# One expert's tokens turned by TensorE instead of by DMA, and its weight splits moved back, in a clustered attention with a mixture of experts

## The chip, the cores and the metric

The kernel runs on one core of a Trainium2 chip, as one launch. The metric is the device time of an execution in microseconds. A core has TensorE (products of matrices, results in PSUM), VectorE, ScalarE and GpSimd (in the profile DVE, ACT and POOL), SyncE (SP), which issues most DMAs here, and 16 DMA engines. Each engine works through its own instructions in order; they meet by semaphores.

## The reference

Two parts in a row. First attention for 2 batches, 8 heads, 768 positions and 64 columns. Each query and key is given to the nearest of 16 centroids, and a query sees only keys of its own cluster:

```python
mask = q_assign[:, :, :, None] == k_assign[:, :, None, :]
scores = np.where(mask, scale * np.matmul(q, k.transpose(0, 1, 3, 2)), -1e9)
attn = softmax(scores)                 # along the keys
x = (attn @ v) as (2, 768, 512)        # the heads side by side
```

Then a mixture of 8 experts, one for each token, chosen by a gate that can also hand on the choice of the token before:

```python
logits = x @ w_gate                    # 512 -> 8
e = argmax(logits[s]) if s == 0 or local_gate[s] < 0.5 else e of token s-1
h = relu(x[s] @ w1[e])                 # 512 -> 1024
out[s] = softmax(logits[s])[e] * (h @ w2[e])   # 1024 -> 512
```

## The kernel before

**Number format.** Every f32 factor of the second part is split into a high and a low f16 half, and a product is three f16 products (high by high, high by low, low by high) summed in PSUM. So a chunk of weights that a DMA has loaded (`wst`, 128 x 1024 f32, 512 KB) needs a *split*: ScalarE writes the high half (L858), then VectorE the low half (L860, `W<-wst,W`). W1 and W2 of an expert are four chunks each.

**Stages.** Attention fills the first 255 us or so. Its tokens are written to DRAM (`xd`) as pairs of f16 halves, and are routed. Tokens are then sorted by expert: the *lead* is the expert with most tokens in the first batch and is done in two parts (200 and 144 slots), the others follow by rank, in the order 1, 7, 2, 6, 3, 5, 4 (`ORD`), with 296, 144, 272, 168, 224, 184 and 200 slots. For each, `expert` (from L882) gives four kinds of work:

- `gather`: GpSimd fetches the rows of the tokens by indirect DMAs of up to 128 rows (L901, `xg`). They must be turned, columns to partitions (`XT`). For the ranks SyncE does this by a DMA transpose for each block (L906). For the lead's second part TensorE does it, by eight transposes for a block (L914, into `xgt` in PSUM), and ScalarE copies the result (L916): that is `turn`.
- `g1(m)`, eight *hidden blocks*: 12 products each (four rows of weights by three, L927 to L929), then ScalarE writes the high half of the hidden values (`H`, L930) and VectorE the low half (L931). Three PSUM buffers hold them.
- `g2`, the *second products*: for a remainder of tokens in two halves of 48 products (L967 to L969, `g2m` and `g2o`), copied by VectorE (`yt`, L970) and turned back by TensorE (L979); for a full 128 tokens in one unit (L948 to L950).
- `put`: ScalarE scales the result (`ob`, L936) and GpSimd scatters it to the output (L938).

**Order.** The program is written in one order, and a scheduler that plans with times of its own sets the order of each engine from it. Behind the lead's first part the loop over `p` does it: at `p` = 0 the hidden blocks and second products of the lead's second part, and spread among them as `tasks` the four splits of rank 1's W1; each split's `two` also issues the next load (`dma_next`). `POST` = 1 says behind how many units the tasks begin. Five loads are issued ahead of the loop (`NST` = 5, the number of `wst` buffers); the later ones wait until a split has freed a buffer. `issue_after` holds an instruction behind a named one.

In the same stretch VectorE and TensorE also do routing work for tokens that overflow their expert's slots: `hbo`, `rbo` (L782 to L788), the slot masks `loj` (L792) and the small products `po` (L793).

Of the kernel before, what the change touches and what calls it, by code (L numbers as in the profile page):

```python
# [43 lines left out]
NST = 5  # L44
ORD = [1, 7, 2, 6, 3, 5, 4]
# [4 lines left out]
POST = 1  # L50
# [9 lines left out]
CAPS = [296, 272, 224, 200, 184, 168, 144]  # L60
# [3 lines left out]
def tile_kernel(ctx, tc, q, k, v, centroids, w_gate, w_local, w1, w2, out):  # L64
    nc = tc.nc
    V, A, G, PE, SP = nc.vector, nc.scalar, nc.gpsimd, nc.tensor, nc.sync
# [10 lines left out]
    E, DM = w1.shape[0], w1.shape[1]  # L77
    DF = w1.shape[2]
    KD, KF = DM // 128, DF // 128
# [9 lines left out]
    xd = dram.tile([B * S, KD, 2, 128], F16, name="xd")  # L89
# [4 lines left out]
    TM, TX = ("pst" if UNI else "pm"), ("pst" if UNI > 1 else "x")  # L94
# [417 lines left out]
    cmark = {}  # L512
# [366 lines left out]
    def expert(r, cap, src, gi, sci, pr, mp, nbuf, g1pool=None, last=False, gates=None, putm=None, tpe=None):  # L879
# [11 lines left out]
        nb = (cap + 127) // 128  # L891
# [13 lines left out]
                else:  # L905
                    cmark["XT"] = SP.dma_start_transpose(out=st["XT"][:, :, i * 128:i * 128 + n], in_=xg[0:n]).ins  # L906

        def turn():
            for i in range(nb):
                n = min(128, pad - i * 128)  # L910
                pool, tag = tpe[i % 2]
                pt = pool.tile([128, 2 * KD, 128], F16, name="xgt", tag=tag)
                for c in range(2 * KD):
                    PE.transpose(pt[:, c, 0:n], st["xg", i][0:n, c * 128:(c + 1) * 128], rc["ident16"][0:n, 0:n])  # L914
                XT = st["XT"][:, :, i * 128:i * 128 + n]
                A.activation(out=XT, in_=pt[:, :, 0:n], func=AF.Copy)  # L916

        def g1(m):
            def f():
# [34 lines left out]
        def g2_rest(h):  # L954
            def f():
                Hh, W2 = st["H"], W[r, 1]
                sl = slice(nf * 128, cap)
                if h == 0:
                    st["yt"] = mp.tile([128, KD, 192], F32, name="yt", tag="yt", bufs=1)
                y = g2_ps()  # L960
                yv = y.rearrange("p (k c) -> p k c", k=2)
                for k2 in range(2):
                    kk = 2 * h + k2
                    for m in range(KF):
                        lh, ll = (W2[:, x, m, kk * 128:(kk + 1) * 128] for x in range(2))
                        with gate(3 * rest / 2400):
                            PE.matmul(out=yv[:, k2, 0:rest], lhsT=lh, rhs=Hh[:, 0, m, sl], start=(m == 0), stop=False)  # L967
                            PE.matmul(out=yv[:, k2, 0:rest], lhsT=lh, rhs=Hh[:, 1, m, sl], start=False, stop=False)
                            PE.matmul(out=yv[:, k2, 0:rest], lhsT=ll, rhs=Hh[:, 0, m, sl], start=False, stop=(m == KF - 1))  # L969
                mark["V"] = V.tensor_copy(st["yt"][:, 2 * h:2 * h + 2, 0:rest], yv[:, :, 0:rest]).ins  # L970
            return f

# [9 lines left out]
        second = []  # L982
# [4 lines left out]
            fl = [flip(i) for i in range(nf, nb)]  # L987
            second = second[:2] + fl + second[2:] if last else second[:3] + fl + second[3:]
        if tpe:
            return gather, [g1(m) for m in range(KF)], second, turn  # L990
        return gather, [g1(m) for m in range(KF)], second

    if True:
# [182 lines left out]
        for f in ea[2]:  # L1176
            f()
        with tc.issue_after(cmark["flip"]):
            eb[3]()
        att.close()  # L1180
        mp = ctx.enter_context(tc.tile_pool(name="mp", bufs=1, side="right"))
        mpool["b"] = mp
# [5 lines left out]
        def dma_next():  # L1188
            if queue:
                r, kd, i = queue.pop(0)  # L1190
                if (r, 0) not in ws:
                    regs[r] = SP.value_load(rc["eid_i"][0:1, r:r + 1], min_val=0, max_val=E - 1)
                if i == 0:
                    ws[r, kd] = wload(r, kd, lambda: regs[r])
                ws[r, kd][i][0]()
        for i in range(NST):
            dma_next()
        col2 = lambda nm, r: (lambda i: rc[nm][:, BASE[r - 1] + i:BASE[r - 1] + i + 1])

        def two(r, kd, i, gather=None):  # L1200
            ws[r, kd][i][1]()
            with tc.issue_after(gather) if gather else nullcontext():
                dma_next()
        ex = [eb]
        mark["on"] = True
        for p in range(E + 1):
            tasks = []
            if p + 1 < E:
                r = ORD[p]
                ex.append(expert(r, CAPS[r - 1], xd, col2("gi", r), col2("sci", r), col2("pr", r), mp, 2, last=p + 1 == E - 1))  # L1210
                ex[-1][0]()
                first.setdefault("XT", cmark["XT"])
            if 0 < p < E:
                tasks += [lambda i=i, r=ORD[p - 1]: two(r, 1, i, first["XT"]) for i in range(4)]
            if p + 1 < E:
                tasks += [lambda i=i, r=ORD[p]: two(r, 0, i, first["XT"]) for i in range(4)]
            units = []
            if p < E:
                units += ex[p][1]

            if p != 1:
                units += ex[max(p - 1, 0)][2]
            nt = 0
            for i, un in enumerate(units):
                un()
                while nt < len(tasks) and nt < (i + 1 - POST) * len(tasks) / (len(units) - POST):
                    tasks[nt]()
                    nt += 1
                if p == E - 1 and i == 0:
                    last_put = mark["G"]  # L1230
                if p == 0 and i == 1:
                    probs()
                if p == 1 and i == 1:
                    late["pool"] = mp
                    over()
# [45 lines left out]
```

## Time and profile before

| | us |
|---|---|
| three executions | 440.75, 443.43, 553.84 (median 443.43) |
| profiled execution | 440.79 |
| its span, first to last instruction | 439.0 |
| TensorE busy | 383.5 (87%) |
| VectorE, ScalarE, GpSimd busy | 300.6, 249.2, 191.3 |

The span is what the trace covers; about 1.8 us of the execution lie around it. Starts in the rows are in us from the start of the span. In a row of instructions the bracket at its end gives how long the engine was idle before it, and what ended that. "Issue" is a wait for nothing that the profile shows, "remote" one that nothing on the core is seen to end. The attention ends near 256 us, the lead's first part near 276, its second part near 299, and rank 1's products begin at 292.

### The profile page before, as it was taken

The numbers are of one execution on the slowest core, as the hardware profiler recorded it, in microseconds if no ns is written. First come the engines' busy times: TensorE is split into PE (matmuls) and PEld (weight loads), VectorE is DVE, ScalarE is ACT, GpSimd is POOL, SyncE is SP. The second block draws the span as 40 slices with busy tenths as digits, with TensorE's granted clock in tenths as the row PEclk, the third lists the DMA queues.
The fourth block names the chain that finished last, engine by engine and source line by source line (L and its number), as shares of the span: only waits on it lengthen the run. The fifth ranks groups of instructions, "written<-read, shape, count | busy, mean of one in ns | idle before, by whom it ended". The sixth has DMA issues, their size and how long they took to land. (4 is left out here: it accounts for less than half of the span.)

```text
span 439.0 us, 12733 instructions
## 1 busy us (share of the span) xinstructions
PE 383.5 (87%) x5095; PEld 336.9 (77%) x5095; DVE 300.6 (68%) x738; ACT 249.2 (57%) x472; POOL 191.3 (44%) x209
## 2 busy tenths in 40 slices
PE   0288698998979999899989999789999999999980
PEld 0246588887979899798879997576799998988950
DVE  7786667765837769879889258848677875876620
ACT  6257867875756667545765520435457756756520
POOL 3005776967739685455667401432133231202120
PEclk9999889999989999799999999999999999999996
DMA  8899879996598949237691710989799999798210
GB/s 195 148 200 266 208 130 194 192 209 149 124 202 160 192 92 197 49 75 172 180 232 21 152 37 20 331 203 227 259 268 327 296 378 305 244 325 250 88 36 32
DMA packets 123166, 80.84 MB, mean 184 GB/s; under 512 B 92503, under 2 KB 108119, under 8 KB 123104
## 3 DMA queue, kind: packets, MB, share of 16 engines
q1 hardware_dynamic: 120480, 73.01, 69.6%
q0 software_dynamic: 2624, 6.98, 4.8%
q8 instruction: 41, 0.67, 0.6%
q14 instruction: 21, 0.17, 0.1%
HBM read 46.88 MB, written 8.47 MB: 126 GB/s over the span
## 5 line engine op out<-in xcount | busy, mean ns | idle before, releaser
L366 POOL TENSOR_TENSOR lo<-e 128x512 f16<-128x512 f32 x90 | 97.1, 1094 | 76.6 <-ACT e L360 76.4
L328 DVE TENSOR_REDUCE mx<-pm 128x2 f32<-128x512 f32 x144 | 96.0, 685 | 33.4 <-PE pm L326 33.0
L360 ACT ACTIVATE e<-pst 128x512 f32<-128x512 f32 x144 | 81.7, 592 | 32.9 <-PE pst L358 27.9
L860 DVE SCALAR_TENSOR_TENSOR W<-wst,W 128x1024 f16<-128x1024 f32 x64 | 78.1, 1230 | 16.7 <-ACT W L858 14.8
L357 PE MATMUL pst<-Q1T,K1T 128*128 128x256 f16 x288 | 73.6, 279 | 4.6 <-ACT e L360 4.2
L358 PE MATMUL pst<-Q2T,K2T 128*128 128x256 f16 x288 | 72.9, 279 | 0.0
L858 ACT ACTIVATE W<-wst 128x1024 f16<-128x1024 f32 x64 | 66.9, 1055 | 7.3 <-DMA wst<-in_moe_w_dram 7.3
L927 PE MATMUL g<-XT,W 128*128 128x200 f16 (+6 forms) x288 | 67.9, 251 | 2.9 <-DMA XT<-xg 1.8
L928 PE MATMUL g<-XT,W 128*128 128x200 f16 (+6 forms) x288 | 67.9, 251 | 0.0
L326 PE MATMUL pm<-K2T,QMT 128*128 128x256 f16 x288 | 58.0, 294 | 10.8 <-DMA QMT<-QM 7.1
L929 PE MATMUL g<-XT,W 128*128 128x200 f16 (+6 forms) x288 | 65.7, 251 | 0.5 <-DVE W L860 0.5
L385 PE MATMUL o<-VF,e 128*128 128x65 f32 x432 | 58.7, 276 | 0.0
L385 PEld LDWEIGHTS o<-VF,e 128*128 128x128 f32 x432 | 55.5, 198 | 0.8
L930 ACT ACTIVATE H<-g 128x200 f16<-128x200 f32 (+6 forms) x72 | 23.6, 339 | 56.7 <-PE g L929 48.2
L938 POOL DMA_INDIRECT out_dram<-ob,scim x16 | 19.0, 1190 | 72.1 <-ACT W L858 19.2
L388 PE MATMUL o<-VL,e 128*128 128x64 f16 x360 | 47.9, 194 | 0.0
L387 PE MATMUL o<-VH,e 128*128 128x65 f16 x360 | 47.9, 196 | 0.0
L389 PE MATMUL o<-VH,lo 128*128 128x65 f16 x360 | 44.9, 195 | 0.4 <-POOL lo L366 0.4
L326 PEld LDWEIGHTS <-QMT 128*128 128x128 f16 x288 | 24.4, 106 | 18.8 <-issue 8.0
L389 PEld LDWEIGHTS <-lo 128*128 128x128 f16 x360 | 34.2, 99 | 2.6 <-issue 1.5
L387 PEld LDWEIGHTS <-e 128*128 128x128 bf16 x360 | 34.7, 99 | 1.8
L388 PEld LDWEIGHTS <-e 128*128 128x128 bf16 x360 | 34.3, 100 | 1.4
(306 smaller groups left out, 882.8 us busy)
## 6 DMA issues: line engine op xcount, KB each, us to landing
wst<-in_moe_w_dram SPq DMA_DIRECT2D x64, 512.0 KB
xd<-xt SPq DMA_DIRECT2D x12, 384.0 KB
ld_k<-in_k_dram SPq DMA_DIRECT2D x7, 384.0 KB
ld_q<-in_q_dram SPq DMA_DIRECT2D x7, 384.0 KB
ld_v<-in_v_dram SPq DMA_DIRECT2D x7, 384.0 KB
Q1T<-QXT SPq DMA_DIRECT2D x14, 192.0 KB
ld_k<-in_k_dram SPq DMA_DIRECT2D x2, 192.0 KB
ld_q<-in_q_dram SPq DMA_DIRECT2D x2, 192.0 KB
```

What stands on the lines that cost most here:

```text
L326: PE.matmul(out=ps[:, i], lhsT=rg(QMT, u)[:, hh * T + 2 * qp + i, :], rhs=rg(K2T, u)[:, hh * T + 2 * kc:hh * T + 2 * kc + 2, :], start=Tru ...
L328: mark["V"] = V.tensor_reduce(out=st["mx"][:, 2 * qp:2 * qp + 2, kc], in_=ps, axis=AX.X, op=ALU.max).ins
L357: PE.matmul(out=ps[:, i], lhsT=rg(K1T, u)[:, j, :], rhs=rg(Q1T, u)[:, hh * T + 2 * qc:hh * T + 2 * qc + 2, :], start=True, stop=False)
L358: PE.matmul(out=ps[:, i], lhsT=rg(K2T, u)[:, j, :], rhs=rg(Q2T, g)[:, 2 * qc:2 * qc + 2, :], start=False, stop=True)
L360: mark["A"] = A.activation(out=e, in_=ps.rearrange("p a b -> p (a b)"), func=AF.Exp, scale=SCL).ins
L366: G.tensor_tensor(out=lo, in0=e, in1=eh, op=ALU.subtract)
L385: PE.matmul(out=o[:, t, 0:65], lhsT=e[:, sl], rhs=vf[:, hh, j, 0:65], start=first, stop=False, skip_group_check=True)
L387: PE.matmul(out=o[:, t, 0:65], lhsT=eh[:, sl], rhs=vh[:, hh, j, 0:65], start=first, stop=False, skip_group_check=True)
L388: PE.matmul(out=o[:, t, 0:64], lhsT=eh[:, sl], rhs=vl[:, hh, j, :], start=False, stop=False, skip_group_check=True)
L389: PE.matmul(out=o[:, t, 0:65], lhsT=lo[:, sl], rhs=vh[:, hh, j, 0:65], start=False, stop=False, skip_group_check=True)
L860: V.scalar_tensor_tensor(out=l[:, cs], in0=s[:, cs], scalar=WS, in1=h[:, cs], op0=ALU.mult, op1=ALU.subtract)
L927: PE.matmul(out=ps, lhsT=lh, rhs=XT[:, 2 * kk, 0:cap], start=(kk == 0), stop=False)
```

## The change

Rank 1's tokens are turned by TensorE and ScalarE, as the lead's second part's are. Its three blocks (128, 128 and 48 rows) give 24 transposes and three copies. The first block's transposes are placed behind the first half of the second products of the lead's second part, the others behind the second half and its turning back, each held behind the last of the second products issued so far. At `p` = 0 the tasks begin behind six units instead of one. Four loads are issued ahead of the loop, and the first task issues two more; the loads at `p` = 0 are no longer held behind a DMA transpose.

```diff
-        def turn():
-            for i in range(nb):
+        def turn(i):
+            def f():
                 n = min(128, pad - i * 128)
-                pool, tag = tpe[i % 2]
+                pool, tag = tpe[i % len(tpe)]
                 pt = pool.tile([128, 2 * KD, 128], F16, name="xgt", tag=tag)
                 for c in range(2 * KD):
                     PE.transpose(pt[:, c, 0:n], st["xg", i][0:n, c * 128:(c + 1) * 128], rc["ident16"][0:n, 0:n])
                 XT = st["XT"][:, :, i * 128:i * 128 + n]
                 A.activation(out=XT, in_=pt[:, :, 0:n], func=AF.Copy)
+            return f
...
-        for i in range(NST):
+        for i in range(NST - 1):
             dma_next()
...
             ws[r, kd][i][1]()
+            if (r, kd, i) == (ORD[0], 0, 0):
+                dma_next()
...
-                ex.append(expert(r, CAPS[r - 1], xd, col2("gi", r), col2("sci", r), col2("pr", r), mp, 2, last=p + 1 == E - 1))
+                ex.append(expert(r, CAPS[r - 1], xd, col2("gi", r), col2("sci", r), col2("pr", r), mp, 2, last=p + 1 == E - 1, tpe=((ps_x, TX), (ps_m, TM)) if p == 0 else None))
...
-                tasks += [lambda i=i, r=ORD[p]: two(r, 0, i, first["XT"]) for i in range(4)]
+                tasks += [lambda i=i, r=ORD[p]: two(r, 0, i, first.get("XT")) for i in range(4)]
...
+            if p == 0:
+                def held(f):
+                    def h():
+                        with tc.issue_after(cmark["g2"]):
+                            f()
+                    return h
+                tu = [held(f) for f in ex[1][3]]
+                units = units[:9] + tu[:1] + units[9:] + tu[1:]
+            post = POST if p else 6
             nt = 0
             for i, un in enumerate(units):
                 un()
-                while nt < len(tasks) and nt < (i + 1 - POST) * len(tasks) / (len(units) - POST):
+                while nt < len(tasks) and nt < (i + 1 - post) * len(tasks) / (len(units) - post):
```

What the scheduler made of it, at three places. The first is ScalarE at the lead's second part and the start of rank 1; `H<-` with 144 columns is a hidden block of the lead's second part, with 296 one of rank 1, `W_5397<-wst` a split of rank 1's W1. Before:

```order
L930 ACTIVATE H<-g_5435 128x144
L858 ACTIVATE W_5397<-wst 128x1024
L930 ACTIVATE H<-g_5475 128x144
L930 ACTIVATE H<-g_5490 128x144
L858 ACTIVATE W_5397<-wst 128x1024
L930 ACTIVATE H<-g_5509 128x144
L930 ACTIVATE H<-g_5524 128x144
L930 ACTIVATE H<-g_5539 128x144
L858 ACTIVATE W_5397<-wst 128x1024
L930 ACTIVATE H<-g_5558 128x144
L858 ACTIVATE W_5397<-wst 128x1024
L936 ACTIVATE ob<-g2m,prlb_4993 128x512
```

And in the changed kernel, from its seventh hidden block on:

```order
L931 ACTIVATE H<-g_5525 128x144
L858 ACTIVATE W_5397<-wst 128x1024
L931 ACTIVATE H<-g_5547 128x144
L858 ACTIVATE W_5397<-wst 128x1024 x2
L916 ACTIVATE XT<-xgt 128x8x128 x2
L916 ACTIVATE XT<-xgt 128x8x48
L937 ACTIVATE ob<-g2m,prlb_4993 128x512
L937 ACTIVATE ob<-g2o,prlb_5003 16x512
L858 ACTIVATE W_5397<-wst 128x1024
L931 ACTIVATE H<-g_5743 128x296
```

The splits stood behind the second, the fourth, the seventh and the eighth hidden block. Now the first stands behind the seventh, two behind the eighth, and the fourth behind the three new copies and two output copies.

The second is VectorE in the same stretch. Before:

```order
L784 TENSOR_TENSOR rbo<-hbo,tok_489 128x12x19
L788 TENSOR_TENSOR rbo<-hbo,vals_525 128x6x19
L931 SCALAR_TENSOR_TENSOR H<-g_5509,H 128x144
L788 TENSOR_TENSOR rbo<-hbo,vals_525 128x6x19
L788 TENSOR_TENSOR rbo<-hbo,vals_526 128x6x19 x2
L931 SCALAR_TENSOR_TENSOR H<-g_5524,H 128x144
L931 SCALAR_TENSOR_TENSOR H<-g_5539,H 128x144
L860 SCALAR_TENSOR_TENSOR W_5397<-wst,W_5397 128x1024
L931 SCALAR_TENSOR_TENSOR H<-g_5558,H 128x144
L970 COPY yt<-g2m 128x2x144
L970 COPY yt<-g2o 128x2x144
L860 SCALAR_TENSOR_TENSOR W_5397<-wst,W_5397 128x1024
```

In the changed kernel:

```order
L788 TENSOR_TENSOR rbo<-hbo,vals_525 128x6x19 x2
L788 TENSOR_TENSOR rbo<-hbo,vals_526 128x6x19 x2
L932 SCALAR_TENSOR_TENSOR H<-g_5480,H 128x144
L932 SCALAR_TENSOR_TENSOR H<-g_5495,H 128x144
L932 SCALAR_TENSOR_TENSOR H<-g_5510,H 128x144
L932 SCALAR_TENSOR_TENSOR H<-g_5525,H 128x144
L860 SCALAR_TENSOR_TENSOR W_5397<-wst,W_5397 128x1024
L932 SCALAR_TENSOR_TENSOR H<-g_5547,H 128x144
L971 COPY yt<-g2m 128x2x144
L860 SCALAR_TENSOR_TENSOR W_5397<-wst,W_5397 128x1024
L971 COPY yt<-g2o 128x2x144
L860 SCALAR_TENSOR_TENSOR W_5397<-wst,W_5397 128x1024 x2
```

The low half of the fourth hidden block (`g_5490` before, `g_5480` now) has moved behind all `rbo`, and that of the eighth (`g_5558`, `g_5547`) stands behind the first split.

The third is SyncE behind the first loads (`eidi` is the list of experts, read into a register). Before:

```order
L844 DMA wst<-in_moe_w_dram 128x2x512
L906 DMA_TRANSPOSE XT<-xg 128x8x128 x2
L906 DMA_TRANSPOSE XT<-xg 128x8x48
L844 ISA
L844 DMA wst<-in_moe_w_dram 128x2x512
L844 ISA
L844 DMA wst<-in_moe_w_dram 128x2x512
```

In the changed kernel:

```order
L844 DMA wst<-in_moe_w_dram 128x2x512
L1194 TENSOR_LOAD eidi
L1194 ISA x2
L844 ISA
L844 DMA wst<-in_moe_w_dram 128x2x512
L906 DMA_TRANSPOSE XT<-xg 128x8x128
L844 ISA
L844 DMA wst<-in_moe_w_dram 128x2x512
L906 DMA_TRANSPOSE XT<-xg 128x8x16
L844 ISA
L844 DMA wst<-in_moe_w_dram 128x2x512
```

The first row is the fifth load in both. Rank 1's three transposes are gone, and the two of rank 7 (128 and 16 rows) stand between the next loads.

## Rows read from the trace of the kernel before

**Rows 1.** The page: the span, and each engine's busy time, share and instructions.

```profile
span 439.0 us, 12733 instructions
PE 383.5 (87%) x5095; PEld 336.9 (77%) x5095; DVE 300.6 (68%) x738; ACT 249.2 (57%) x472; POOL 191.3 (44%) x209
```

**Rows 2.** By stretch: its length, busy PE, PEld, DVE, ACT, POOL; clock, DMA, GB/s.

```profile
302.00:426.00 124.00, 124.00 (x1466) 109.15 (x1464) 85.18 (x130) 74.41 (x121) 29.59 (x25) 1.00 0.83 257
```

**Rows 3.** The same view, the stretch that the change rewrites.

```profile
280.00:302.00 22.00, 16.83 (x214) 14.31 (x211) 12.23 (x40) 8.06 (x16) 6.88 (x8) 1.00 0.95 237
```

**Rows 4.** TensorE in order of time, 276 to 302: start, duration, line, operation, [idle before].

```profile
276.00 0.90 PE L914 MATMUL xgt<-ident,xg 128*128 128x128 f16 x16
...
279.64 0.46 PE L729 MATMUL pp<-rb,ohlo 128*128 128x32 f16 x12
...
281.01 0.23 PE L929 MATMUL g<-XT,W 128*128 128x144 f16 x1
...
285.17 0.22 PE L967 MATMUL g2m<-H,W 128*128 128x144 f16 x1 [1.58 <-ACT H L930]
...
288.30 0.23 PE L927 MATMUL g<-XT,W 128*128 128x144 f16 x1
...
288.98 0.23 PE L929 MATMUL g<-XT,W 128*128 128x144 f16 x1
...
292.15 0.30 PE L927 MATMUL g<-XT,W 128*128 128x296 f16 x1 [1.82 <-DMA XT<-xg]
...
294.81 0.29 PE L928 MATMUL g<-XT,W 128*128 128x296 f16 x1
...
300.03 0.43 PE L929 MATMUL g<-XT,W 128*128 128x296 f16 x2 [0.48 <-DVE W L860]
...
301.52 0.29 PE L927 MATMUL g<-XT,W 128*128 128x296 f16 x1 [0.31 <-DVE H L931]
```

**Rows 5.** ScalarE in order of time, the same stretch.

```profile
280.06 1.06 ACT L858 ACTIVATE W<-wst 128x1024 f16<-128x1024 f32 x1
284.83 0.47 ACT L930 ACTIVATE H<-g 128x144 f16<-128x144 f32 x2 [3.71 <-remote]
...
299.42 0.69 ACT L936 ACTIVATE ob<-g2m,prlb 128x512 f32<-128x512 f32 x1 [8.93 <-issue]
```

**Rows 6.** VectorE in order of time, 282 to 291.

```profile
282.61 0.17 DVE L609 TENSOR_SCALAR p0m<-pp 128x16 f32<-128x16 f32 x1 [1.65 <-PE g L929]
...
285.16 0.31 DVE L931 SCALAR_TENSOR_TENSOR H<-g,H 128x144 f16<-128x144 f32 x1 [0.47 <-ACT H L930]
...
285.67 0.17 DVE L806 CAST oei<-oe 128x19 int32<-128x19 f32 x1
...
286.28 1.23 DVE L860 SCALAR_TENSOR_TENSOR W<-wst,W 128x1024 f16<-128x1024 f32 x1
...
288.13 0.64 DVE L788 TENSOR_TENSOR rbo<-hbo,vals 128x114 f16<-128x114 f16 x3
...
289.39 1.23 DVE L860 SCALAR_TENSOR_TENSOR W<-wst,W 128x1024 f16<-128x1024 f32 x1 [0.18 <-ACT W L858]
```

**Rows 7.** By stretch again, one us inside the burst of loads and gathers.

```profile
282.00:283.00 1.00, 0.67 (x9) 0.46 (x7) 0.39 (x3) 0.00 (x0) 0.74 (x1) 1.00 1.08 422
```

**Rows 8.** SyncE's DMA issues in order of time: start, time in its queue, count.

```profile
276.09 0.53 SPq L844 DMA_DIRECT2D wst<-in_moe_w_dram  x1
285.97 4.61 SPq L906 DMA_TRANSPOSE XT<-xg  x3
290.84 1.63 SPq L844 DMA_DIRECT2D wst<-in_moe_w_dram  x3
```

**Rows 9.** The tile `xgt`, 260 to 312: durations in ns, shortest/median/longest, and forms.

```profile
L914 PE MATMUL xgt<-ident,xg x16: 164/198/219, 276.0 to 276.7; 128*128 128x128 f16 x8, 16*128 16x16 f16 x8
L916 ACT ACTIVATE XT<-xgt x2: 276/646/1015, 276.9 to 277.8; 128x1024 f16<-128x1024 f16 x1, 128x128 f16<-128x128 f16 x1
```

**Rows 10.** GpSimd in order of time: the next gather that needs a free buffer.

```profile
291.02 0.88 POOL L901 DMA_INDIRECT xg<-xd,gim  x1 [4.29 <-DMA XT<-xg]
```

More of the change, by code (lines that the diff above doesn't have):

```diff
@@ L968, in f @@
                             PE.matmul(out=yv[:, k2, 0:rest], lhsT=lh, rhs=Hh[:, 1, m, sl], start=False, stop=False)
-                            PE.matmul(out=yv[:, k2, 0:rest], lhsT=ll, rhs=Hh[:, 0, m, sl], start=False, stop=(m == KF - 1))
+                            cmark["g2"] = PE.matmul(out=yv[:, k2, 0:rest], lhsT=ll, rhs=Hh[:, 0, m, sl], start=False, stop=(m == KF - 1)).ins
                 mark["V"] = V.tensor_copy(st["yt"][:, 2 * h:2 * h + 2, 0:rest], yv[:, :, 0:rest]).ins
@@ L989, in expert @@
         if tpe:
-            return gather, [g1(m) for m in range(KF)], second, turn
+            return gather, [g1(m) for m in range(KF)], second, [turn(i) for i in range(nb)]
         return gather, [g1(m) for m in range(KF)], second
@@ L1178, in tile_kernel @@
         with tc.issue_after(cmark["flip"]):
-            eb[3]()
+            for f in eb[3]:
+                f()
         att.close()
@@ L1209, in tile_kernel @@
                 r = ORD[p]
-                ex.append(expert(r, CAPS[r - 1], xd, col2("gi", r), col2("sci", r), col2("pr", r), mp, 2, last=p + 1 == E - 1))
+                ex.append(expert(r, CAPS[r - 1], xd, col2("gi", r), col2("sci", r), col2("pr", r), mp, 2, last=p + 1 == E - 1, tpe=((ps_x, TX), (ps_m, TM)) if p == 0 else None))
                 ex[-1][0]()
-                first.setdefault("XT", cmark["XT"])
+                if p:
+                    first.setdefault("XT", cmark["XT"])
             if 0 < p < E:
@@ L1222, in tile_kernel @@
                 units += ex[max(p - 1, 0)][2]
+            if p == 0:
+                def held(f):
+                    def h():
+                        with tc.issue_after(cmark["g2"]):
+                            f()
+                    return h
+                tu = [held(f) for f in ex[1][3]]
+                units = units[:9] + tu[:1] + units[9:] + tu[1:]
+            post = POST if p else 6
             nt = 0
```

## The prediction, made before the change was run

> **What bounds the kernel now.** I read the page first: TensorE is busy for 87% of the span, more than any other engine [rows 1]. The second view is busy time by stretch. From 302 to 426 us TensorE has no idle time at all, at a granted clock of 1.00 (the upper of its two levels, 2.4 GHz), while DMA stands at 0.83 [rows 2]. So whatever is gained or lost before 302 us is carried to the end one for one, and from 302 on only TensorE's own work could change the time. That work does not change: the same products follow in nearly the same order.
>
> The third view is the waits of TensorE between 280 and 302 us, the stretch that the change rewrites. TensorE is busy for 16.83 of 22 us [rows 3]. Its longest stops: 1.58 us for a hidden block that ScalarE had not copied, 1.82 us for the DMA transposes of the first rank, 0.48 us for the last split of W1, 0.31 us for VectorE [rows 4].
>
> The first of these stops has an odd cause. TensorE's record of the third hidden block ends at 281.24 [rows 4], yet ScalarE starts its copy at 284.83 after 3.71 us of waiting for which the trace names nobody on the core [rows 5], and VectorE waited 1.65 us, until 282.61, for products that TensorE's record ends at 280.1 [rows 4, 6]. TensorE's signals reached both engines about 2.5 and 3.5 us late while DMA ran at 1.08 of its engines and 422 GB/s [rows 7]. I see no other stop like it.
>
> **Where the reckoning ends.** My mark is the start of the first rank's third product block, 301.52 [rows 4]. Before it both kernels do the same products, and behind it the same. The sum is the shift of this mark, added to the profiled execution's 440.79 us (span 439.0 and 1.8 around it). The three runs shown have their median at 443.43, 0.6% above the profiled execution, so the median can lie up to 2.6 us over the sum.
>
> **The change part by part.**
>
> *Four first loads instead of five.* SyncE's order shows the same five loads in a row in both kernels, for the fifth has a free buffer and nothing to wait for. Worth 0. They are the burst, with four gathers, in which the signals come late; it stays where it was, and so, I take it, does the lateness.
>
> *Three DMA transposes leave SyncE's queue.* They held it for 4.61 us from 285.97, and the next loads stood behind them until 290.84 [rows 8]. These loads now wait for VectorE's splits instead, which end later (below), so nothing comes sooner. The 1.82 us wait goes.
>
> *24 transposes come onto TensorE.* The lead's 16 took 0.90 us from first to last [rows 4], 0.056 each, so 24 cost 1.35 us. As a bound from the other side: if each had to run alone at its median of 198 ns [rows 9], 4.75 us. I take 1.35, because the 16 are the same instruction on the same tile. The Trainium skill's "TensorE: Matmul & The Clock Gate", section "Part 4: PE-mode transpose", gives about 275 ns for one inside a kernel; by that 24 would cost 6.6 us (an estimate from that page). The trace disagrees: 0.90 us for 16.
>
> *ScalarE copies them.* 1.015 us for a full block [rows 9]; the 48 columns of the last one by the line between the two sizes there, 0.49.
>
> *The splits of W1 move behind the hidden blocks.* One split is 1.06 on ScalarE and 1.23 on VectorE [rows 5, 6]. In the old order three of four were done by 290.6, in time that TensorE did not ask for. Now the first stands between the seventh and the eighth hidden block on both engines, and the fourth behind the last transposed copy and two output copies.
>
> **The sum, with the signals late as before.** A block of 12 products on 144 tokens is 0.75 us (0.062 each, 288.30 to 288.98 for 11 steps); one product on 296 tokens is 0.127 (292.15 to 294.81, 21 steps) [rows 4, 9].
>
> 1. ScalarE resumes at 284.83, VectorE has the low half at 285.46 [rows 6], TensorE goes on at 285.5 with the sixth block. It did the fifth in the gap, for no split's order is in its way there; before, it resumed at 285.17 with the fifth. Gain 0.75 less 0.3: 0.45.
> 2. The sixth block and 8 second products end at 286.75. The seventh needs the low half of the fourth, and this now stands behind seven routing operations. In the old order these ran from 285.67 to 288.8 with a split (1.15 from start to start) and a low half (0.2) between them [rows 6]: 1.7 us. So it comes at 287.4. Loss 0.65.
> 3. The seventh and eighth blocks and 23 second products end at 290.4. But ScalarE's first split runs from 288.7 to 289.75, the eighth copy follows until 290.0, VectorE's split ends at 291.0 and the eighth low half at 291.25; 52 second products stand behind it. Loss 0.9.
> 4. 52 second products (3.25), 24 transposes (1.35) and the 8 turns back that were there before (1.3) end at 297.2. The last transposed copy ends on ScalarE at 297.7. Loss 0.5, where 1.82 us stood before.
> 5. 17 products take until 299.9. ScalarE's two output copies (0.69 for one [rows 5], 1.3 together, the second being of 16 rows) and the fourth split end at 300.05, VectorE's at 301.3. TensorE waits 0.15 and 0.6, where 0.48 stood before, and goes on with the fourth weight row at 301.3 instead of 300.03.
> 6. From there to the mark it took 1.5 us, with VectorE's slot masks between; VectorE now begins them behind the split as it did then. The mark falls at 302.8.
>
> Checked the other way: gained 0.45 + 1.82 + 0.48 = 2.75; lost 1.35 + 0.65 + 0.9 + 0.5 + 0.75 = 4.15; the shift is +1.4, against +1.3 by the clock. **Forecast: 440.8 + 1.3 = 442.1 us.** No change that can be told: about 2%, or 8.8 us, is what a measurement of this kernel can tell.
>
> **Rivals.**
>
> *The signals come in time* (25%). For it: the lateness is one event in one execution, and the split that lay beside it on ScalarE is gone. Against: loads and gathers of the burst stand unchanged. The third copy then starts near 281.3, the low half of the third block is done near 282.1 behind VectorE's routing, the sixth block starts at 283.2, the seventh waits for nothing, and the 52 second products start at 288.35 instead of 291.3. All behind comes 2.95 sooner: 442.1 less 2.95, 439.2 us.
>
> *The new waits are all hidden* (7%): the engines slip past each other, so that steps 2 to 5 cost nothing but the transposes. Late signals: 440.8 - 2.75 + 1.35 = 439.4; signals in time as well: 2.3 less (the sixth block at 283.2 instead of 285.5), 437.1.
>
> *The last chunk of W2 comes late, and the kernel is slower* (8%). Place: SyncE's queue. The third load there after the first five now waits for VectorE's third split (296.7, behind the copy of the second half of the outputs, instead of 290.6 [rows 6]) and stands behind a transposition of rank 7 whose gather waits for the new transposes to free a buffer; POOL waited in this manner before, until 291.02, for the DMA transposes [rows 10]. It goes out near 299.5, where the old one left by 292.5 [rows 8]. Its split is wanted near 306. It decides if landing takes over 6.5 us. The fifth first load left at 276.09 [rows 8], and 6 us later the DMA engines were still full [rows 7]; I allow up to 9 us in a burst. Price: what goes over, 2.5 us at most, so 444.6. Against: with three DMA transposes fewer the engines are freer.
>
> *The transposes run one by one* (4%): 4.75 instead of 1.35 on TensorE, 442.1 + 3.4 = 445.5. By the Trainium skill's price for one (the same page and section) it would be 442.1 + 5.25 = 447.3, an estimate. Against: the lead's 16.
>
> **Chances and range.** Forecast 56%, the rivals 25, 7, 8 and 4%. The range takes in the second case (439.2, and somewhat below for the third) and the late chunk (444.6), and for the forecast the 2.6 us by which the median of runs lay over the profiled execution: 437.5 to 445.5. Faster by over 2% would need more than the 5.2 us that TensorE idles in the whole stretch: 3%. Slower by over 2% would need two of the mishaps at once, or one that I don't see: 3%. Within 2%: 94%.
>
> **What would show it.** Right: no wait for DMA transposes before the first rank's products; 24 transposes on TensorE in 1.3 to 1.6 us; a stop of some 0.9 us before the 52 second products that VectorE ends, with a split just before; the mark 2 to 3 us later than the 52 would allow because of ScalarE's last copy and VectorE's fourth split; TensorE full behind it. The second case shows as a third copy on ScalarE near 281.3 instead of 284.8. Wrong would be idle time of TensorE behind 303 us, above all before the second products of the first rank, or a mark before 299.

## The result, and the profile after

The changed kernel took 436.55 us in the median of four runs (435.53 to 437.05). The kernel before, over its four, took 442.09 (440.22 to 553.84). The ratio, which leaves out slow runs, is 0.9867, with a 95% interval from 0.9834 to 0.9901. My forecast was 442.1 with a range from 437.5 to 445.5, so the time fell below the range.

Three of the kernel before's four times are those shown ahead of the prediction, taken before the changed kernel ran, so how much of this 1.3% belongs to the change has to come from the runs below. They show two kinds of batches (a batch is what ran on one chip, one kernel after the other, with the kernel before among them). In one kind the profiles show TensorE's signals late, as in the profile that I predicted from, and the change is worth nothing: 1.0005 [0.9969, 1.0040] and 1.0008 [0.9969, 1.0046]. In the other the signals come in time, and it is worth about 1%: 0.9905 [0.9873, 0.9938] and 0.9910 [0.9870, 0.9951].

The page of the changed kernel, its first lines (engine: busy us, share of the span, instructions):

```profile
span 434.6 us, 12777 instructions
PE 378.6 (87%) x5119; PEld 333.9 (77%) x5119; DVE 298.5 (69%) x738; ACT 251.7 (58%) x475; POOL 193.4 (45%) x209
```

The profiled execution took 436.38 us, the profiled one before 440.79. Behind 302 us TensorE still has no idle time, which is the answer to [rows 2]. Busy time by stretch: busy us of each engine and its instructions, then the granted clock, the share of the DMA engines and GB/s.

```profile
302.00:422.00 120.00, 120.00 (x1428) 105.91 (x1426) 81.23 (x125) 70.86 (x115) 26.74 (x22) 1.00 0.86 260
```

TensorE in the changed stretch, from the routing product `pt` to the mark, with all of its stops over 0.5 us and those that the prediction names (start, duration, instruction, and in the bracket the idle time before it and what ended it). It answers to [rows 4]:

```profile
275.66 0.45 PE L719 MATMUL pt<-rb,ohlo 128*128 128x16 f16 x12 [0.47 <-DVE rb L713]
...
286.43 0.22 PE L969 MATMUL g2m<-H,W 128*128 128x144 f16 x1 [0.59 <-DVE H L932]
...
288.05 0.61 PE L914 MATMUL xgt<-ident,xg 128*128 128x128 f16 x8
...
290.56 0.91 PE L914 MATMUL xgt<-ident,xg 128*128 128x128 f16 x16
...
292.67 0.29 PE L928 MATMUL g<-XT,W 128*128 128x296 f16 x1 [0.61 <-ACT XT L916]
...
295.99 0.43 PE L930 MATMUL g<-XT,W 128*128 128x296 f16 x2 [0.34 <-DVE W L860]
...
297.33 0.29 PE L928 MATMUL g<-XT,W 128*128 128x296 f16 x1 [0.17 <-DVE H L932]
```

The last row is the mark. It stands 297.33 - 275.66 = 21.67 us behind the start of `pt`; before it stood 301.52 - 277.34 = 24.18 behind [rows 4]. The waits that steps 3 to 5 foretold are there, in their places and with the engines that were named (of step 5's two only VectorE's), but the 1.58 us stop for a hidden block is gone. The two engines that had waited for late signals show why. ScalarE's third copy, then VectorE's `p0m`, to be read beside [rows 5] and [rows 6]:

```profile
279.50 0.29 ACT L931 ACTIVATE H<-g 128x144 f16<-128x144 f32 x1 [1.07 <-PE g L930]
```

```profile
279.11 0.16 DVE L609 TENSOR_SCALAR p0m<-pp 128x16 f32<-128x16 f32 x1
```

The third copy starts 3.84 us behind `pt`; before it was 7.49. `p0m` waits for nothing at all.

The two profiles differ by 4.41 us. Of these 277.34 - 275.66 = 1.68 lie ahead of `pt`, where the change touches nothing: in two later profiles of the changed kernel itself `pt` starts at 278.48 and at 275.48. Between `pt` and the mark lie 24.18 - 21.67 = 2.51, behind the mark (439.0 - 301.52) - (434.6 - 297.33) = 0.21.

### The profile page after: what moved, and what is told of

Read it like the earlier page. It is cut to its first block, busy times and chain, and to the rows that moved or that the text cites. A ratio compares the mean times of both kernels' runs of the same rounds, so it can differ in the third digit from the quotient of the medians.

```text
span 434.6 us, 12777 instructions
## 1 busy us (share of the span) xinstructions
PE 378.6 (87%) x5119; PEld 333.9 (77%) x5119; DVE 298.5 (69%) x738; ACT 251.7 (58%) x475; POOL 193.4 (45%) x209
## 5 line engine op out<-in xcount | busy, mean ns | idle before, releaser
L366 POOL TENSOR_TENSOR lo<-e 128x512 f16<-128x512 f32 x90 | 95.5, 1077 | 74.4 <-ACT e L360 74.2
L860 DVE SCALAR_TENSOR_TENSOR W<-wst,W 128x1024 f16<-128x1024 f32 x64 | 79.2, 1246 | 20.9 <-ACT W L858 20.5
L357 PE MATMUL pst<-Q1T,K1T 128*128 128x256 f16 x288 | 71.8, 274 | 4.2 <-ACT e L360 3.6
L358 PE MATMUL pst<-Q2T,K2T 128*128 128x256 f16 x288 | 71.1, 273 | 0.6 <-DMA Q2T<-Q 0.6
L326 PE MATMUL pm<-K2T,QMT 128*128 128x256 f16 x288 | 57.0, 289 | 13.3 <-DMA QMT<-QM 8.3
L385 PE MATMUL o<-VF,e 128*128 128x65 f32 x432 | 56.7, 270 | 0.0
L385 PEld LDWEIGHTS o<-VF,e 128*128 128x128 f32 x432 | 53.4, 192 | 0.7
L387 PE MATMUL o<-VH,e 128*128 128x65 f16 x360 | 46.9, 194 | 0.0
L932 DVE SCALAR_TENSOR_TENSOR H<-g,H 128x200 f16<-128x200 f32 (+6 forms) x72 | 25.3, 363 | 15.3 <-ACT H L931 14.8
L387 PEld LDWEIGHTS <-e 128*128 128x128 bf16 x360 | 34.0, 98 | 1.5
```

Source lines behind the costliest of these rows:

```text
L326: PE.matmul(out=ps[:, i], lhsT=rg(QMT, u)[:, hh * T + 2 * qp + i, :], rhs=rg(K2T, u)[:, hh * T + 2 * kc:hh * T + 2 * kc + 2, :], start=Tru ...
L357: PE.matmul(out=ps[:, i], lhsT=rg(K1T, u)[:, j, :], rhs=rg(Q1T, u)[:, hh * T + 2 * qc:hh * T + 2 * qc + 2, :], start=True, stop=False)
L358: PE.matmul(out=ps[:, i], lhsT=rg(K2T, u)[:, j, :], rhs=rg(Q2T, g)[:, 2 * qc:2 * qc + 2, :], start=False, stop=True)
L366: G.tensor_tensor(out=lo, in0=e, in1=eh, op=ALU.subtract)
L385: PE.matmul(out=o[:, t, 0:65], lhsT=e[:, sl], rhs=vf[:, hh, j, 0:65], start=first, stop=False, skip_group_check=True)
L387: PE.matmul(out=o[:, t, 0:65], lhsT=eh[:, sl], rhs=vh[:, hh, j, 0:65], start=first, stop=False, skip_group_check=True)
```

## The experiments

Theory A: the lateness of the signals belongs to the old order (its splits, its DMA transposes, or the burst of loads and gathers). Theory B: it was one event in one execution. Later ones are named as they come. The first batch put the parts of the change apart.

**Loads only.** Four first loads and nothing else. The scheduler gives every engine the order of the kernel before.

```diff
-        for i in range(NST):
+        for i in range(NST - 1):
             dma_next()
...
             ws[r, kd][i][1]()
+            if (r, kd, i) == (ORD[0], 0, 0):
+                dma_next()
```

> Only the four first loads instead of five; the order of instructions on every engine is that of the kernel before, row for row. So its time is the kernel before's (ratio 0.995 to 1.005) by both theories, and its profile is a second look at the kernel before. Theory A (the late signals of TensorE are a steady cost of the old order): the third hidden block's copy on ScalarE again starts 3 to 4 us after TensorE's record of that block ends. Theory B (one event in one execution): it starts within 0.3 us of the record, and TensorE is busy for some 19 us of the 22 before the first rank's third product block instead of 16.8.

Measured: 440.01 us, ratio 1.0021 [0.9985, 1.0056]. The third copy waited again:

```profile
282.64 0.47 ACT L930 ACTIVATE H<-g 128x144 f16<-128x144 f32 x2 [3.75 <-remote]
```

It starts 282.64 - 275.13 = 7.51 us behind `pt`, against 7.49 before. One event in one execution does not repeat to 0.02 us: theory B falls.

**Splits early.** The changed kernel with `POST` at `p` = 0 as it was; TensorE's transposes stay. Three splits then stand behind the second, fifth and eighth hidden block, and the fourth behind the new copies and the first output copy.

```diff
-            post = POST if p else 6
+            post = POST
```

> The change with the four splits of the first rank's W1 back at their old places among the hidden blocks; the 24 transposes on TensorE stay. Theory A with the splits as the cause (a split on ScalarE and VectorE beside the burst of loads goes with the late signals): the lateness of 2.5 to 3.5 us is back, and the kernel loses about 2.3 us to the changed one: 438.5 to 440. Theory A with the DMA transposes as the cause: signals in time, time as the changed kernel's or up to 1 us shorter, since the waits for the first split (0.59) and the fourth go: 435.5 to 437. Theory B: as the latter.

Measured: 440.06 us, 1.0014 [0.9980, 1.0049]; third copy late (3.72 us, "remote"). Rank 1's DMA transposes are gone here, so they do not make the signals late.

**Late splits only.** The kernel before with the splits placed as in the change; DMA transposes stay.

```diff
-                while nt < len(tasks) and nt < (i + 1 - POST) * len(tasks) / (len(units) - POST):
+                while nt < len(tasks) and nt < (i + 1 - (POST if p else 6)) * len(tasks) / (len(units) - (POST if p else 6)):
```

> The kernel before with the four splits placed late and nothing else; the three DMA transposes of the first rank stay. Theory A with the splits as the cause: signals in time (third copy within 0.3 us of TensorE's record), 2.3 us gained there, 0.6 lost before the second products: near 440. Theory A with the DMA transposes as the cause: the third copy starts 3 us late again, and the time is 441.5 to 443. Theory B: signals in time, but the wait for the DMA transposes (1.8 us or more, as TensorE arrives there earlier) stays: 440 to 442, no difference that can be told from the kernel before.

Measured: 442.28 us, 1.0055 [1.0022, 1.0089]: slower by half a per cent. The third copy is late again (4.67 us), so the early splits do not make the signals late either.

**The kernel before, unchanged**, for a third profile.

> The kernel before once more, for a third profile of it. Theory A: third copy on ScalarE 3 to 4 us behind TensorE's record again. Theory B: within 0.3 us. The time is 440 to 444 by both.

Measured: 439.02 us; third copy 3.72 us late, 7.48 us behind `pt`. The kernel before over this batch: 440.38 us. So with each part of the change taken out the lateness stays, and only the whole seemed to be without it. The second batch, on another chip, ran the whole again.

**The changed kernel again**, twice (no edit). Theory C: only the changed order has the signals in time. Theory D: it is a matter of the execution.

> The changed kernel itself, once more beside the kernel before. In five profiles of four orders (the kernel before three times, the splits early, the late splits alone) the signals of TensorE came 2 to 3.6 us late at the same place to 0.1 us; in the one profile of the changed kernel they did not. Theory C (the changed order as a whole is what brings them in time): in time again, ratio 0.983 to 0.990. Theory D (the lateness comes and goes by execution or by chip, whatever the order): late here, third copy 3.5 us behind TensorE's record, and the time is that of my forecast's steps, within 0.5% of the kernel before.

> The same once more for a third profile of the changed kernel. Theory C: signals in time. Theory D: as it falls.

Measured: 439.93 us, 1.0005 [0.9969, 1.0040], and 442.64 us in the single run. The signals were late in both profiles. From the first, ScalarE:

```profile
283.98 0.47 ACT L931 ACTIVATE H<-g 128x144 f16<-128x144 f32 x2 [4.74 <-remote]
```

and TensorE:

```profile
276.47 0.45 PE L719 MATMUL pt<-rb,ohlo 128*128 128x16 f16 x12 [0.47 <-DVE rb L713]
...
291.21 0.22 PE L969 MATMUL g2m<-H,W 128*128 128x144 f16 x1 [0.59 <-DVE H L932]
...
297.45 0.29 PE L928 MATMUL g<-XT,W 128*128 128x296 f16 x1 [0.61 <-ACT XT L916]
...
300.77 0.42 PE L930 MATMUL g<-XT,W 128*128 128x296 f16 x2 [0.34 <-DVE W L860]
...
302.11 0.29 PE L928 MATMUL g<-XT,W 128*128 128x296 f16 x1 [0.17 <-DVE H L932]
```

The same program as in the first section, with the same waits of 0.59, 0.61 and 0.34 us, and the mark 25.64 us behind `pt` (24.57 in the other profile) instead of 21.67. Theory C falls. The change as I had reckoned it, with late signals, is what this batch shows.

The lateness is not in the signals alone. In this profile TensorE itself stands idle again and again behind 281 us, "for issue":

```profile
282.46 0.22 PE L969 MATMUL g2o<-H,W 128*128 128x144 f16 x1 [0.38 <-issue]
...
283.19 0.24 PE L930 MATMUL g<-XT,W 128*128 128x144 f16 x1 [0.32 <-issue]
...
283.92 0.23 PE L928 MATMUL g<-XT,W 128*128 128x144 f16 x1 [0.48 <-issue]
```

Such stops, two to six of 0.18 to 1.06 us between 4.5 and 10 us behind `pt`, stand in all eleven profiles with late signals, and in none of the nine with signals in time.

**Three first loads**, the kernel before otherwise (`range(NST)` becomes `range(NST - 2)`), and **plain loads**, which tried the burst and the gathers as causes:

> The kernel before with three first loads instead of five, so that the burst moves 1 MB less before and beside the gathers. If the burst of loads makes TensorE's signals late: in time here, with the DMA engines below 0.8 beside the third and fourth gather. If not: pp's signal again 0.7 us behind the start of the third gather, the third block's 1.75 us behind that of the fourth. Time 440 to 443 (a load fewer in flight brings the splits later).

```diff
+                if r == ORD[0]:
+                    cmark["xg"] = SP.dma_start(out=xg[0:n], in_=src[i * 128:i * 128 + n].rearrange("s k a c -> s (k a c)")).ins
+                else:
                     cmark["xg"] = G.indirect_dma_start(out=xg[0:n], ...
```

> The kernel before with the first rank's three gathers replaced by three plain loads of as many rows on SyncE's queue (other rows than the routing asks, so that rank computes on other tokens). POOL then issues one gather in that stretch instead of four. If POOL's gathers make TensorE's signals late: in time here, and the stretch some 2 us shorter (437 to 439). If the burst of loads does it: late as before, 439 to 442.

Measured: 439.84 and 441.57 us, both with late signals, 5.12 and 5.21 us of "remote" wait at the third copy:

```profile
283.99 0.50 ACT L930 ACTIVATE H<-g 128x144 f16<-128x144 f32 x2 [5.12 <-remote]
```

```profile
286.27 0.47 ACT L933 ACTIVATE H<-g 128x144 f16<-128x144 f32 x2 [5.21 <-remote]
```

With three loads the DMA engines had room beside the third and fourth gather, and the signals were late; in the changed kernel's first profile they were full, and the signals in time. The same stretch of the two, three loads first:

```profile
279.63:281.76 2.13, 1.14 (x12) 0.74 (x12) 1.41 (x4) 0.00 (x0) 1.82 (x2) 1.00 0.59 170
```

```profile
280.09:282.34 2.25, 2.25 (x39) 2.25 (x37) 2.19 (x11) 0.58 (x2) 1.94 (x2) 1.00 1.05 414
```

So it is not the burst. The plain loads missed their aim: GpSimd took the next ranks' gathers forward into the place, and issued four there as before (0.97, 1.13, 0.96 and 0.94 us). But the first profile of the changed kernel has four gathers too, from 277.29 to 282.34, and no lateness; they don't make the signals late by themselves. Theory A has no cause left of those that I had named.

**A third batch**, two profiles of each kernel, no edits:

> The kernel before, fourth profile. Theory D (whether TensorE's signals come late is a matter of the execution, not of the order): late (pp's signal 1.8 to 2.5 us behind the end of its record, about 440 us) or in time (all signals within 0.02 us, and then about 3 us less in the stretch: 436 to 437.5). Theory C (only the changed order can have them in time): late.

> The changed kernel, fourth profile, and five rounds beside the kernel before. Theory D: the ratio to the kernel before is 0.996 to 1.004 whatever the signals do, since both have them alike on one chip; by my steps the mark lies 0.3 to 1.4 us later behind pt than in the kernel before when both are late. Theory C: ratio 0.983 to 0.990.

> As the first of this group, a fifth profile of the kernel before.

> As the second of this group, a fifth profile of the changed kernel: in time by theory C's last chance only if both of its profiles here are and the two of the kernel before are not.

Measured: the kernel before 442.95 and 442.17 us (median over the batch 442.5), the changed one 437.87 us, 0.9905 [0.9873, 0.9938], and 437.13. Signals in time in all four profiles, on the chip of the second batch, where all four had them late. So the lateness belongs to neither kernel, nor to a chip: theory D holds on that, with the addition that all profiles of a batch are alike. But what it said of the ratio was wrong, and this is what I had not reckoned with. The kernel before, with signals in time, is *slower*. Its second profile here, ScalarE's third copy and then TensorE:

```profile
279.80 0.29 ACT L930 ACTIVATE H<-g 128x144 f16<-128x144 f32 x1
```

```profile
275.96 0.45 PE L719 MATMUL pt<-rb,ohlo 128*128 128x16 f16 x12 [0.47 <-DVE rb L713]
...
291.55 0.43 PE L927 MATMUL g<-XT,W 128*128 128x296 f16 x1 [5.26 <-DMA XT<-xg]
291.77 0.45 PE L928 MATMUL g<-XT,W 128*128 128x296 f16 x1
...
295.63 0.29 PE L927 MATMUL g<-XT,W 128*128 128x296 f16 x1
295.76 0.29 PE L928 MATMUL g<-XT,W 128*128 128x296 f16 x1
...
302.85 0.29 PE L927 MATMUL g<-XT,W 128*128 128x296 f16 x1 [0.32 <-DVE H L931]
```

and the same stretch by time (the column before the last two is the granted clock):

```profile
286.40:291.40 5.00, 0.00 (x0) 0.00 (x0) 0.37 (x2) 0.04 (x1) 0.15 (x1) 0.73 1.08 162
291.40:293.40 2.00, 1.85 (x8) 1.19 (x9) 0.00 (x0) 0.00 (x0) 1.69 (x2) 0.50 0.93 262
293.40:295.40 2.00, 2.00 (x10) 1.22 (x9) 0.00 (x0) 0.00 (x0) 0.96 (x2) 0.50 1.02 307
```

TensorE comes to rank 1's first product early, and stands there for 5.26 us until the DMA transposes have landed. In the profile that I predicted from it stood for 1.58 us at the hidden block and then for 1.82 here [rows 4], because it came later. The transposes land at nearly the same time in both kinds: rank 1's first product starts 14.8 to 15.6 us behind `pt` in all nine profiles in which rank 1 is turned by DMA. So late signals cost the kernel before next to nothing: they fall into a wait that it has anyway. The changed kernel has no such wait, and there the first product starts at 17.0 with signals in time and at 19.9 to 21.6 with late ones.

Behind the stop the granted clock is 0.50 (the 1.2 GHz level): from 291.55 to 295.48 products follow each other every 0.247 us, later every 0.126. 3.93 us at half the pace lose 1.9. The mark stands 302.85 - 275.96 = 26.89 us behind `pt`, 2.7 later than in the profile that I predicted from. The other profile has a shorter wait, and its mark at 25.93:

```profile
292.48 0.43 PE L927 MATMUL g<-XT,W 128*128 128x296 f16 x1 [4.81 <-DMA XT<-xg]
```

Theory E: the transposes on TensorE bring the gain, by taking this wait and the fall of the clock away. Its rival F: the early splits, beside which two of the gathers took 1.45 and 2.68 us instead of 0.88 and 0.96 (the last section has the rows). **The fourth batch**, on a third chip, had signals in time too and tells them apart; the edits are those above.

> TensorE's transposes with the splits at their old places, once more. If the signals are in time here (as in the last four profiles): by theory E (with signals in time the kernel before loses 5 us to the DMA transposes, 5.26 of waiting and then TensorE at its lower clock level) the transposes alone bring nearly all of the gain: ratio to the kernel before 0.988 to 0.993, no stop of TensorE over 1.5 us behind pt. By its rival F (the early splits beside the gathers are the loss): ratio 0.997 to 1.002. If the signals are late: 0.998 to 1.005, as before.

> The late splits alone, with the DMA transposes, once more. Signals in time: by theory E TensorE again stops some 5 us for the DMA transposes and falls to the lower clock level: ratio 0.998 to 1.006. By F the gathers are free of the splits, the transposes land 1 to 2 us sooner, and the ratio is 0.990 to 0.995. Signals late: 1.002 to 1.009, as before.

> The changed kernel beside the three above, on the same chip. Signals in time: ratio 0.987 to 0.994 to the kernel before. Late: 0.997 to 1.004.

Measured: transposes on TensorE with the splits early 436.56 us, 0.9882 [0.9845, 0.9918]; late splits with the DMA transposes 443.94 us, 1.0051 [1.0009, 1.0093]; the changed kernel 437.48 us, 0.9910 [0.9870, 0.9951]. The late splits alone, TensorE and the stretch by time:

```profile
292.15 0.33 PE L927 MATMUL g<-XT,W 128*128 128x296 f16 x1 [4.85 <-DMA XT<-xg]
```

```profile
292.10:294.10 2.00, 1.95 (x9) 1.26 (x10) 0.00 (x0) 0.00 (x0) 1.43 (x2) 0.55 0.72 149
294.10:296.10 2.00, 2.00 (x20) 1.81 (x19) 0.00 (x0) 0.00 (x0) 0.50 (x1) 0.60 0.81 125
```

The transposes alone, TensorE's longest stop in the stretch, and the third gather:

```profile
292.54 0.29 PE L928 MATMUL g<-XT,W 128*128 128x296 f16 x1 [0.60 <-ACT XT L916]
```

```profile
280.59 1.45 POOL L901 DMA_INDIRECT xg<-xd,gim  x1 [0.30 <-issue]
```

The third gather is slow there as well (the fourth took 1.04), and it costs nothing; TensorE's granted clock stays at 1.00 through the stretch. In the late splits alone both gathers are quick (0.88 and 1.06 us) and the stop is there all the same, so F falls. Theory E holds: the transposes are the whole gain, within the intervals, and the late splits by themselves are a loss of half a per cent in both kinds of batches (1.0055 and 1.0051).

**A row of four.** The two waits that the new order still has (0.59 for the eighth low half, 0.34 for the fourth split) come from where the splits stand. This version puts all four behind the eighth hidden block:

```diff
-                while nt < len(tasks) and nt < (i + 1 - post) * len(tasks) / (len(units) - post):
+                while nt < len(tasks) and nt < (((i >= 7) * len(tasks)) if p == 0 else (i + 1 - post) * len(tasks) / (len(units) - post)):
```

> The changed kernel with its four splits in one row behind the eighth hidden block, instead of one ahead of it, two behind and one behind the output copies. The waits of my steps 3 and 5 (0.59 and 0.34 measured) should go, the others stay: 0.8 to 1.0 us less than the changed kernel, whether the signals are late or not; that is 0.2%, at the edge of what five rounds can tell. If ScalarE's row of four holds up the first transposed copy, or VectorE's the flipped rows, nothing is won.

> The row of four splits again, now against the changed kernel on one chip. From the profiles the stretch behind pt is 1.5 us shorter than the changed kernel's: with signals in time 1.0 to 1.8 us less than the next run, ratio to the kernel before near 0.988. With signals late: 0.5 to 1.5 us less than the next run, 0.996 to 1.000 to the kernel before.

> The changed kernel as measure of the run before it: ratio to the kernel before 0.987 to 0.994 with signals in time, 0.997 to 1.004 with late ones.

Measured in the fourth batch: 436.23 us, 0.9889 [0.9828, 0.9950]. The row stands on ScalarE in one piece, and both waits are gone, as is the one for the last transposed copy; one for VectorE's copy of the outputs comes instead:

```profile
285.82 3.90 ACT L858 ACTIVATE W<-wst 128x1024 f16<-128x1024 f32 x4
```

```profile
292.33 0.44 PE L980 MATMUL g2m<-ident,yt 128*128 128x128 f32 x2 [0.45 <-DVE yt L971]
```

In a fifth batch, with late signals again (4.67 us at the third copy), it took 441.02 us, 1.0008 [0.9967, 1.0050], and the changed kernel 441.32 us, 1.0008 [0.9969, 1.0046]. In both batches its median is lower than the changed kernel's, by 1.25 us (0.8 to 1.0 was expected) and 0.3 (0.5 to 1.5), but the intervals overlap, and by the table below it is the slower one in its only late profile: that it is better is not shown.

The profiles together, as the time from the start of `pt` to the end of the span, which leaves out the attention's own scatter (the kernel before with signals late stands there with the loads-only run, whose order is the same, as its second):

| us behind `pt` | signals late | signals in time |
|---|---|---|
| kernel before | 161.7, 162.3, 162.1 | 163.9, 164.4 |
| changed kernel | 163.2, 162.3, 163.7 | 158.9, 159.3, 159.1, 159.1 |
| transposes on TensorE, splits early | 161.9 | 158.6 |
| late splits, DMA transposes | 163.3 | 165.4 |
| row of four | 165.6 | 157.6 |
| three first loads; plain loads | 162.9; 162.5 | |

## Why the prediction was wrong

**What failed is the premise of the sum, "the signals late as before".** I argued it in the part on the loads: the burst "stays where it was, and so, I take it, does the lateness". The burst stayed, and in two of the five later batches, as in the changed kernel's first profile, the lateness was not there. With three loads in the burst instead of five, with the splits moved, with the DMA transposes gone, it was there all the same. I gave "the signals come in time" 25%, as something that the change might bring about. It is nothing that either kernel does.

As I had priced it, that case lies inside the range, at 439.2. The changed kernel's medians in the two later batches with signals in time, 437.87 and 437.48, stand at its lower edge, and the first one, 436.55, lies 0.95 us below. Of what parts the first profiled execution from that case, 1.68 us lie ahead of `pt`, where nothing was changed; they are scatter. The rest is a price that was too high (below).

**For late signals the sum was near, in part by luck.** It put the mark 302.8 - 277.34 = 25.46 us behind `pt`; the three late profiles have 25.64, 24.57 and 26.23. In the first and the last of them the granted clock fell to 0.51 to 0.64 for about 4 us, which the sum did not have; the one at full clock has its mark 0.89 us ahead of the sum, with waits of 0.59, 0.61 and 0.34 us for steps 3 to 5 instead of 0.9, 0.5 and 0.75. The sum made +1.3 us, or 0.3%; the ratio of that batch, 1.0005 [0.9969, 1.0040], holds it, and no change.

**The rival "signals in time" had the right mechanism and the wrong size.** Its third copy, near 281.3, and its 52 second products, at 288.35, are 3.96 and 11.01 us behind `pt`; measured are 3.84 and 10.77. Its time was 439.2, and the profiled execution took 436.38. From one to the other: the 52 products start 0.24 sooner, with step 3's wait at 0.59 instead of 0.9; from there to rank 1's first product it is 6.24 instead of 6.4; from that to the fourth weight row 3.32 instead of 3.6, with step 5's wait at 0.34 instead of 0.75; from 295.99 to the mark 1.34 instead of 1.5. That is 0.24 + 0.16 + 0.28 + 0.16 = 0.84. With the 0.21 behind the mark and the 1.68 ahead of `pt`, 2.73 in all, 439.15 less 2.73 is 436.42.

**What no case of mine had: the price of the DMA transposes.** I took it from the row, 1.82 us. That was what the late signals had left of it to be seen. The same kernel with signals in time waits 4.81 and 5.26 us for them, and in the second profile it loses 1.9 more at the lower clock level. So I compared the changed kernel with signals in time to the kernel before with late ones, and missed that this rival makes the kernel before slower.

**Step by step otherwise.** Four first loads: worth 0, and the order is the same, as said. The transposes: their rows are 0.61 and 0.91 long, and TensorE went on to the next product 0.45 and 0.84 us behind their start (288.50 and 291.40), so the 24 cost 1.29, where the sum had 1.35. That price was taken from 16 of which eight are of 16 columns only [rows 9], so that it came out so well is partly luck. By the 275 ns of the Trainium skill ("TensorE: Matmul & The Clock Gate", Part 4: PE-mode transpose) the 24 would have been 6.6 us, an estimate; the trace disagrees. The late W2 chunk: TensorE has no idle time behind 302 us, so that case did not come. Step 2 (0.65 for the seventh block) is 0.37 in one late profile and nothing in time. The splits' places, which I costed with the rest, are what the change could have done without.

## What to carry to other kernels

A stop that no engine on the core explains may belong to the execution and not to the kernel: before it goes into a sum, look whether a profile of another batch has it (here all profiles of a batch were alike), and make the sum for both kernels with it and without. A stop hides the stop behind it, so the wait that a row shows for a transfer is only what is left of it; reckon when the transfer lands, and when its user would come if nothing else held it. A comparison of two kernels means most where both ran in one batch.

## What the runs showed of the hardware

- TensorE's signals came late in whole batches: in the first profile of the kernel before and in every profile of the first, second and fifth batch they reached ScalarE and VectorE some microseconds behind the end of TensorE's records, and at nearly the same place: the third copy starts 7.44 to 7.51 us behind `pt` in eight of these eleven profiles and 8.19 to 8.97 in three, and TensorE shows the stops "for issue" of the second batch. In the third and fourth batch, one of them on the chip of the second, no signal was late, and the third copy of all nine profiles with signals in time starts at 3.83 or 3.84. The first and the fifth batch ran on one chip. What makes the difference stays open; no run here could set it.
- A gather that GpSimd begins while one of VectorE's splits is running ends late. Over the twenty profiles 129 gathers begin so, and all but one of them end 0.72 to 0.99 us behind the split, a little less than the 0.85 to 1.21 that a gather takes by itself. Of 57 that begin ahead of a split and still run when it begins, 55 take no longer than that. From the kernel before in the third batch, first GpSimd's rows and then VectorE's:

```profile
280.39 1.45 POOL L901 DMA_INDIRECT xg<-xd,gim  x1 [0.31 <-issue]
282.14 2.68 POOL L901 DMA_INDIRECT xg<-xd,gim  x1 [0.30 <-issue]
```

```profile
279.87 1.21 DVE L860 SCALAR_TENSOR_TENSOR W<-wst,W 128x1024 f16<-128x1024 f32 x1
...
282.28 1.21 DVE L860 SCALAR_TENSOR_TENSOR W<-wst,W 128x1024 f16<-128x1024 f32 x1
```

The same gather in the profile that I predicted from begins just ahead of the split and is not slowed:

```profile
283.05 0.96 POOL L901 DMA_INDIRECT xg<-xd,gim  x1 [0.30 <-issue]
```

```profile
283.08 1.23 DVE L860 SCALAR_TENSOR_TENSOR W<-wst,W 128x1024 f16<-128x1024 f32 x1
```

The Trainium skill ("SBUF — State Buffer", Terms) says that VectorE and GpSimd share a pair of ports and that the loser of the two waits for the whole instruction. The gathers that begin inside a split, the one of 1.45 us among them, fit that. The 2.68 us do not: that gather began 0.14 us ahead of the split, and so did the only other one of this length, in the other profile of the same kernel and batch. No run took this apart.
- Stops of TensorE of 4.81 to 5.26 us were followed by a granted clock of 0.50 to 0.60 for 2 to 4 us, and products at up to twice their time. In the six profiles with signals in time that lack this stop the clock stayed at 1.00 through the stretch. But with late signals it fell as well, in seven of eleven profiles, to 0.50 to 0.56 in the lowest stretch of 2 us, between 8 and 14 us behind `pt`. Stops of 1.56 and 1.63 us stood ahead of such a fall, and stops of 1.58 and 1.64 us had none behind them. In the profile whose mark is 25.64 us behind `pt` only the stops "for issue" shown above, none over 0.5 us, stand ahead of 2 us in which TensorE is busy throughout:

```profile
284.92:286.92 2.00, 2.00 (x20) 2.00 (x18) 1.97 (x9) 0.35 (x2) 0.98 (x1) 0.50 0.15 57
```

What decides it, these runs do not show.
